# First batch's attention: the mask enters the scores as a product on TensorE, and the exponentials read PSUM

## The chip, the cores and the metric

The kernel runs on one core of one Trainium2 chip. The metric is the time of one execution on the device in microseconds (us), as the median of several runs. The engines go by the names of the profile: PE is TensorE, PEld its weight loads, DVE is VectorE, ACT is ScalarE, POOL is GpSimd, and SP is the engine on whose queue nearly all transfers are issued.

## What is computed

Three stages follow each other: attention over 4 batches of 8 heads (576 positions, 64 wide) in which a position sees a window of 32 positions, plain for the first four heads and with a stride of 4 for the others, and then two feed-forward layers over the 2304 positions.

```python
scores = q @ k.T / sqrt(64)                     # per batch and head, 576 x 576
scores = where(mask, scores, -1e9)              # windows of 32, plain or strided by 4
attn = exp(scores - max(scores)); attn = attn / (sum(attn) + 1e-9)
x = attn @ v                                    # heads side by side: 2304 x 512
x = ((x @ w_a) * (x @ w_b)) @ w_out             # 512 -> 1536 -> 512
h = x @ w_in                                    # 512 -> 2048
out = (max(h, 0) + alpha * min(h, 0)) @ w_out2  # 2048 -> 512
```

The matrices of the two layers arrive as 64-bit floats and are read as integers; the kernel converts them itself.

## The kernel before

**Attention.** A batch is 12 groups (`B`=4 batches, 4 pairs of heads, 3 groups in each). A group is 3 pieces of 64 queries against 96 keys for two heads, so that scores are a tile of 128x288. `Group` holds its operations: `scores` (12 small products into a PSUM tile `sp`), `largest` (DVE: the `scalar_tensor_tensor` of L345 reads `sp`, scales it by 1/8, adds the mask `mk` and writes `st` in SBUF; then the `tensor_reduce` of L351 takes the negated maximum of each row), `exps` (ACT, L356: three exponentials of 128x96 with that maximum as bias and the row's sum as a second output), `weights` (DVE, L363 to L365: reciprocal and product), `transposed` (PE, L372: three transposes into `tp`), `moved` (ACT, L377: copies `tp` to SBUF), `values` (PE, L385: 12 small products into `ap`) and `placed` (DVE, L410: copies `ap` into the layer's input).

**The first batch** stands alone at the start: group i begins at step i, its weights come one step later, its transposes two, its values three. Its `sp` tiles share the tag `at` with two PSUM buffers; `tp` and `ap` have one buffer each (`acc0`, `acc1`). The later three batches run between the products of the first layer; they share banks by twos (`visit_scores`, tile `sa`) and use the same methods of `Group`.

**Fillers.** Before the first step 11 products of zeros (`heat`, L535, 128x512 in bf16) run on PE, and one more in each of the 17 steps of the start. They write a PSUM tile that nobody reads.

**Loads.** `load_qk(n + 3)` is issued after the scores of group n, `load_v(n + 3)` after its values; each has three places in a ring. `queue` and `belt` hold the conversions of weight matrices: a job loads 512 KB of raw words (L194; `in_wab` for the first layer's two matrices, `in_wo` for the third), ACT and DVE make floats of them (L176 to L186) and split them into a high and a low half (L244 on ACT, L247 on DVE), and a store (L258 `wad`, L268 `wod`) keeps a copy. All of these transfers stand on SP's queue.

**The first layer** starts when enough is there: `contract` multiplies the input by a block of `w_a` into `pa` and of `w_b` into `pb`, `expand` multiplies the product by a block of `w_out` into four accumulators; each is made of triples of 128x128x512 products (L452 to L454).

**Order.** The program is written step by step, and a scheduling layer then sets the order of instructions on each engine when the program is built, so that an instruction may stand before one that was written earlier. Each engine, and SP's queue, works through its own order; an instruction that waits holds up all behind it, except that PE loads weights ahead.

Of the kernel before, what the change touches and what calls it, by code (L numbers as in the profile page):

```python
# [12 lines left out]
BF16 = mybir.dt.bfloat16  # L13
U32 = mybir.dt.uint32
I64 = mybir.dt.int64
AF = mybir.ActivationFunctionType
ALU = mybir.AluOpType
AX = mybir.AxisListType

B, H, S, D = 4, 8, 576, 64  # L20
# [6 lines left out]
KT = QT + WINDOW  # L27
NST = S // QT
GS = 3
KS = GS * QT + WINDOW  # L30
NG = NST // GS
NCLS = S // DILATION
NEG = -1.0e9
TILES = [(0, 512), (512, 512), (1024, 512), (1536, 768)]
N_PLAIN = 3

# [3 lines left out]
MASK_OF = {(0, 0): 0, (0, 1): 1, (0, 2): 1, (1, 0): 2, (1, 1): 3, (1, 2): 4}  # L40


def mask_table():
# [4 lines left out]
    for (dil, g), at in MASK_OF.items():  # L48
        for s in range(GS):
# [3 lines left out]
            if dil:  # L53
                ok &= q // NCLS == k // NCLS
            m = np.where(ok, 0.0, NEG)
            out[:QT, at, s], out[QT:, at, s] = m, m
# [4 lines left out]
def tile_kernel(ctx: ExitStack, tc: tile.TileContext, qk, v, mask, wab, wo1, w2, alpha, out):  # L61
    nc = tc.nc
    keep = ctx.enter_context(tc.tile_pool(name="keep", bufs=1))
# [5 lines left out]
    wad = dram.tile([NFA, 128, 1024], F32, name="wad")  # L69
    wsd = dram.tile([NFB // 2, 7, 128, 512], F32, name="wsd")  # L70
    ident = keep.tile([128, 128], F32, name="ident")
    al = keep.tile([128, NFB], F32, name="al")


# [3 lines left out]
    class Ring:  # L78


        def __init__(self, t, first, size, n):
            self.places = [t[:, first + i * size:first + (i + 1) * size] for i in range(n)]
# [5 lines left out]
    def cut(t, first, *dims):  # L88
        size = int(np.prod(dims))
        ap = t[:, first:first + size]  # L90
        if len(dims) == 2:
            ap = ap.rearrange("p (a b) -> p a b", b=dims[1])
        elif len(dims) == 3:
            ap = ap.rearrange("p (a b c) -> p a b c", b=dims[1], c=dims[2])
        return ap
# [17 lines left out]
    sm_ring = Ring(ft, a0 + 4608, 3 * GS, 4)  # L113
    mk = cut(ft, a0 + 4648, 720).bitcast(BF16).rearrange("p (m k) -> p m k", m=5)
# [26 lines left out]
    before, after, now = {}, {}, [0]  # L141

    def at_step(table, k, fn):
        table.setdefault(k, []).append(fn)
# [140 lines left out]
    def load_qk(n):  # L285
        if n < B * NC * NG:
            tqs[n] = t = qk_ring.next()
            nc.sync.dma_start(out=t, in_=qk[n // (NC * NG), n % (NC * NG)])

    def load_v(n):  # L290
        if n < B * NC * NG:
            tvs[n] = t = v_ring.next()[:KT].rearrange("p (s j d) -> p s j d", j=2, d=D)
            nc.sync.dma_start(out=t, in_=v[n // (NC * NG), n % (NC * NG)])

    class Group:


        def __init__(self, b, i, k=None, lag=None, tags=None):
            self.b, self.n, self.pr, self.g = b, b * NC * NG + i, i // NG, i % NG
            self.id = f"{b}_{i}"  # L300
            self.tags = tags
            self.swap = 0
            self.shared = None
            if k is None:
                return
            at_step(before, k, self.scores)
            at_step(after, k + lag[0], self.largest)
            at_step(after, k + lag[1], self.exps)
            at_step(after, k + lag[2], self.weights)
            at_step(before, k + lag[3], self.transposed)  # L310
            at_step(after, k + lag[3], self.moved)
            at_step(before, k + lag[4], self.values)
            at_step(after, k + lag[4], self.placed)
# [2 lines left out]
            tag, bufs = self.tags[n]  # L316
            return ps.tile([128, 512], F32, tag=tag, bufs=bufs, name=f"{what}{self.id}")

        def scores(self):
            Group.scores_of([self])  # L320

        @staticmethod
        def scores_of(groups):


            for a, group in enumerate(groups):
                group.swap = a
                group.tq = tqs.pop(group.n)
                group.sp = group.psum(0, "sp") if group.shared is None else group.shared
            for s in range(GS):  # L330
                for group in groups:
                    for j in range(2):
                        half, to = (slice(x * 64, (x + 1) * 64) for x in (j, j ^ group.swap))
                        nc.tensor.matmul(
                            group.sp[to, s * KT:(s + 1) * KT],
                            lhsT=group.tq[half, s * QT:(s + 1) * QT],
                            rhs=group.tq[half, GS * QT + s * QT:GS * QT + s * QT + KT],
                            start=True, stop=True,
                        )
            for group in groups:  # L340
                load_qk(group.n + 3)

        def largest(self):
            self.st = st_ring.next().rearrange("p (s k) -> p s k", k=KT)
            nc.vector.scalar_tensor_tensor(  # L345
                out=self.st.rearrange("p s k -> p (s k)"), in0=self.sp[:, :GS * KT], scalar=1.0 / float(D) ** 0.5,
                in1=mk[:, MASK_OF[int(self.pr >= 2), self.g]], op0=ALU.mult, op1=ALU.add,
            )
            self.sp = None
            self.sm = sm_ring.next().rearrange("p (a s) -> p a s", s=GS)  # L350
            nc.vector.tensor_reduce(out=self.sm[:, 0], in_=self.st, axis=AX.X, op=ALU.max, negate=True)  # L351

        def exps(self):
            self.et = et_ring.next().rearrange("p (s k) -> p s k", k=KT)
            for s in range(GS):
                nc.scalar.activation(  # L356
                    self.et[:, s], self.st[:, s], AF.Exp, bias=self.sm[:, 0, s:s + 1], accum_out=self.sm[:, 1, s:s + 1]
                )
            self.st = None

# [112 lines left out]
    def bank(tag):  # L473
        return ps.tile([128, 512], F32, tag=tag, name=tag)
# [22 lines left out]
    load_qk(1)  # L497
    load_v(1)
    make_identity(nc, ident)
    xn[0], xn[1] = cut(ft, 0, 4, 512), cut(ft, 2048, 4, 512)  # L500

    def more():
# [6 lines left out]
    lag = (0, 0, 1, 2, 3)  # L509
# [8 lines left out]
    k = 5  # L518
# [7 lines left out]
                job_o(k, job[3])  # L526
        k += 2 if k < n_start else 1

    zeros = keep.tile([128, 512], BF16, name="zeros")
    nc.vector.memset(zeros, 0.0)  # L530
    idle = bank("pb")

    def heat(n):
        for _ in range(n):
            nc.tensor.matmul(idle, lhsT=zeros[:, :128], rhs=zeros, start=True, stop=True)  # L535

    heat(11)
    for _ in range(n_start):
        step(lambda: heat(1))
    nc.sync.dma_start(out=al, in_=alpha)  # L540
# [37 lines left out]
    for t in range(3):  # L578
# [3 lines left out]
        for j in range(len(pairs) + 1):  # L582
            k = slots[2 * j] if j < len(pairs) else slots[-1] + 2
# [65 lines left out]
    k = start_of[N_PLAIN - 1]  # L649
# [25 lines left out]
    for t, (t0, n) in enumerate(TILES[:N_PLAIN]):  # L675
# [3 lines left out]
        for f in range(NFA):  # L679
# [11 lines left out]
            k = now[0]  # L691
# [233 lines left out]
```

## Time and profile before

| | before |
|---|---|
| median of 3 runs | 913.97 us (912.05 to 916.38) |
| the profiled execution | 919.15 us |
| its span in the profile | 917.1 us |
| PE busy | 895.0 us (98%) |
| DVE busy | 617.4 us (67%) |
| ACT busy | 415.2 us (45%) |
| mean granted TensorE clock over the span | 0.988 of full |

The profiled execution lies 5.2 us above the median. 2.05 us of it lie outside the span. Busy shares are means over the whole program: the first batch's attention is over within some 45 us of the start, and only there, and in the some 25 us after it, PE is idle for more than moments at a time. A busy PE is not a PE at full speed: two clock levels are granted, 2.4 GHz (1.00 in the tables) and 1.2 GHz (0.50).

### The profile page before, as it was taken

How to read it: one execution, taken by the hardware profiler on the slowest of the kernel's cores; microseconds unless marked ns; L12 is line 12 of the kernel's file. 1: busy time of each engine (PE TensorE's matmuls, PEld its weight loads, DVE VectorE, ACT ScalarE, POOL GpSimd, SP SyncE). 2: the span in 40 equal slices, each digit the busy share in tenths (PEclk: the TensorE clock that was granted, in tenths of full speed). 3: DMA queues.
4: the chain of work that ended last, by engine and by line, in shares of the span. 5: the costliest groups of instructions: out<-in, count | busy, mean ns of one | idle time of the engine just before them, and what ended most of it. 6: DMA issues, size and time to landing. Idle time of an engine off the chain costs nothing.

```text
span 917.1 us, 15187 instructions
## 1 busy us (share of the span) xinstructions
PE 895.0 (98%) x5572; PEld 810.7 (88%) x5572; DVE 617.4 (67%) x1317; ACT 415.2 (45%) x967; POOL 0.7 (0%) x6
## 2 busy tenths in 40 slices
PE   8979999999999999999999998999999999999998
PEld 5658888888777778899999998999999999999998
DVE  5788897656766776579877588759555575555442
ACT  5787886545545544345445356224222242222221
POOL 0000000000000000000000000000000000000000
PEclk9899999999999999999999999999999999999999
DMA  7788894687778663663322987557445445454200
GB/s 206 221 297 298 307 336 177 226 267 262 228 240 282 216 204 122 205 206 131 124 93 68 329 288 274 156 157 239 118 118 150 127 115 157 115 146 123 71 35 34
DMA packets 76585, 171.24 MB, mean 187 GB/s; under 512 B 8672, under 2 KB 23776, under 8 KB 76512
## 3 DMA queue, kind: packets, MB, share of 16 engines
q1 hardware_dynamic: 76512, 170.28, 57.5%
q8 instruction: 44, 0.72, 0.3%
q14 instruction: 29, 0.24, 0.1%
HBM read 133.55 MB, written 36.70 MB: 186 GB/s over the span
## 4 chain that ended last, share of the span: by engine, by line
PE 78%; DMA 10%; DVE 5%; ACT 4%; issue 1%; SPq 1%; ACTq 0%; DVEq 0%
PE at L711 12%; PE pb L711 8%; PE pa L711 8%; PE accB L453 7%; PE accB L454 7%; PE accB L452 7%; DMA ft<-in_w 5%; PE accA L452 4%; PE accA L453 4%; PE accA L454 4%; PE pa L452 2%; PE pb L452 2%; PE pb L453 2%; PE pa L454 2%; PE pb L454 2%; PE pa L453 2%
## 5 line engine op out<-in xcount | busy, mean ns | idle before, releaser
L244 ACT CAST rt<-ft 128x512 fp32r<-128x512 f32 (+2 forms) x288 | 159.3, 561 | 280.4 <-PE accB L454 169.1
L247 DVE TENSOR_TENSOR rt<-ft,rt 128x512 fp32r<-128x512 f32 (+2 forms) x288 | 174.8, 613 | 135.0 <-ACT rt L244 121.1
L711 PE MATMUL at<-rt 128*128 128x384 f32 x648 | 130.7, 334 | 1.2 <-DMA rt<-wsd 1.2
L453 PE MATMUL accB<-rt 128*128 128x384 f32 x384 | 128.7, 335 | 0.2 <-DVE rt L247 0.2
L454 PE MATMUL accB<-rt 128*128 128x384 f32 x384 | 128.7, 335 | 0.0
L452 PE MATMUL accB<-rt 128*128 128x384 f32 x384 | 127.8, 335 | 0.0
L711 PEld LDWEIGHTS at<-rt 128*128 128x128 f32 x648 | 113.9, 188 | 1.7 <-DMA rt<-wsd 1.6
L452 PE MATMUL accA<-rt 128*128 128x512 f32 (+1 forms) x240 | 90.0, 379 | 5.7 <-ACT rt L244 4.5
L725 ACT COPY ft<-at 128x384 f32<-128x384 f32 x108 | 51.8, 480 | 89.4 <-PE at L711 87.3
L453 PE MATMUL accA<-rt 128*128 128x512 f32 (+1 forms) x240 | 89.3, 372 | 0.7 <-DVE rt L247 0.7
L711 PE MATMUL pb<-rt 128*128 128x384 f32 x432 | 87.2, 336 | 2.8 <-DVE ft L722 2.8
L454 PE MATMUL accA<-rt 128*128 128x512 f32 (+1 forms) x240 | 88.9, 370 | 0.0
L711 PE MATMUL pa<-rt 128*128 128x384 f32 x432 | 88.1, 337 | 0.0
L711 PEld LDWEIGHTS pb<-rt 128*128 128x128 f32 x432 | 75.6, 188 | 4.6 <-DVE ft L722 4.6
L711 PEld LDWEIGHTS pa<-rt 128*128 128x128 f32 x432 | 76.7, 189 | 0.1
L453 PEld LDWEIGHTS accB<-rt 128*128 128x128 f32 x384 | 72.3, 188 | 0.6 <-DVE rt L247 0.5
L454 PEld LDWEIGHTS accB<-rt 128*128 128x128 f32 x384 | 72.4, 188 | 0.0
L452 PEld LDWEIGHTS accB<-rt 128*128 128x128 f32 x384 | 72.3, 188 | 0.0
L183 DVE SCALAR_TENSOR_TENSOR ft<-ft 128x512 uint32<-128x512 uint32 x68 | 46.8, 688 | 34.9 <-ACT ft L179 34.5
L176 ACT ACTIVATE ft<-ft 128x512 f32<-128x512 f32 x68 | 45.7, 672 | 46.9 <-DMA ft<-in_w 43.3
L356 ACT ACTIVATE ft<-ft 128x96 f32<-128x96 f32 x144 | 52.1, 363 | 20.0 <-DVE ft L351 20.0
L722 DVE TENSOR_TENSOR ft<-ft,pb 128x384 f32<-128x384 f32 x72 | 39.7, 551 | 29.5 <-ACT ft L725 29.2
(80 smaller groups left out, 1351.3 us busy)
## 6 DMA issues: line engine op xcount, KB each, us to landing
rt<-wsd SPq DMA_DIRECT2D x168, 256.0 KB, 2.9
rt<-wod SPq DMA_DIRECT2D x48, 512.0 KB, 4.2
ft<-in_w SPq DMA_DIRECT2D x32, 512.0 KB, 5.1
wsd<-rt SPq DMA_DIRECT2D x56, 256.0 KB, 2.6
ft<-in_wab SPq DMA_DIRECT2D x24, 512.0 KB, 5.4
ft<-in_qk SPq DMA_DIRECT2D x48, 208.0 KB, 4.3
ft<-in_v SPq DMA_DIRECT2D x48, 144.0 KB, 4.2
wad<-ft SPq DMA_DIRECT2D x24, 256.0 KB, 4.7
```

The costliest lines, as they stand in the source:

```text
L176: nc.scalar.activation(f, high.bitcast(F32), AF.Abs, scale=2.0 ** -112)
L183: nc.vector.scalar_tensor_tensor(out=fi, in0=fi, scalar=3, in1=low, op0=ALU.logical_shift_left, op1=ALU.bitwise_or)
L244: hi_eng.copy(hi, x)
L247: lo_eng.tensor_tensor(out=lo, in0=x, in1=hi.bitcast(F32), op=ALU.subtract)
L356: nc.scalar.activation(self.et[:, s], self.st[:, s], AF.Exp, bias=self.sm[:, 0, s:s + 1], accum_out=self.sm[:, 1, s:s + 1])
L452: nc.tensor.matmul(acc, lhsT=wh, rhs=rh, start=first, stop=False)
L453: nc.tensor.matmul(acc, lhsT=wh, rhs=rl, start=False, stop=False)
L454: nc.tensor.matmul(acc, lhsT=wl, rhs=rh, start=False, stop=last)
L711: nc.tensor.matmul(acc[:, :HT], lhsT=a, rhs=x[:, b, c], start=start and c == k == 0, stop=c == 1 and k == 2, skip_group_check=not start,)
L722: nc.vector.tensor_tensor(out=out, in0=x, in1=acc[:, :HT], op=ALU.add)
L725: nc.scalar.copy(out, acc[:, :HT])
```

## The change

Only the first batch changes. The mask no longer enters on DVE: for each of the 12 groups a product of a bf16 identity (`ident_b`) and the mask's 288 columns (bf16, now -8e9 where masked, since the scale of 1/8 comes later) is written into `sp` first, and the 12 score products add to it. The maximum is taken by a `tensor_reduce` straight from `sp` and then scaled by a small `tensor_scalar` of 128x3; L345's pass is gone. The exponentials read `sp` in PSUM, with the scale as an argument, so a bank of `at` is held until the third exponential is done, where it was free after L345. The later batches keep their path (with the other value of `NEG`). The fillers have 384 columns where they had 512, and 14 stand ahead of the first step where 11 stood; `zeros` now shares a tile `few` with `ident_b`, which POOL casts from `ident`.

```diff
-NEG = -1.0e9
+NEG = -8.0e9
+SCALE = 1.0 / float(D) ** 0.5
...
+    few = keep.tile([128, 512], BF16, name="few")
+    ident_b, zeros = few[:, :128], few[:, 128:]
...
-            self.shared = None
+            self.sp = self.shared = None
+            self.scale = 1.0 if k is None else SCALE
             if k is None:
                 return
-            at_step(before, k, self.scores)
-            at_step(after, k + lag[0], self.largest)
+            at_step(before, k, self.masked_scores)
+            at_step(after, k + lag[0], self.largest_masked)
...
-        def scores(self):
+        def masked_scores(self):
+
+            self.sp = self.psum(0, "sp")
+            nc.tensor.matmul(
+                self.sp[:, :GS * KT], lhsT=ident_b, rhs=mk[:, MASK_OF[int(self.pr >= 2), self.g]],
+                start=True, stop=True,
+            )
             Group.scores_of([self])
+
+        def largest_masked(self):
+            self.st = self.sp[:, :GS * KT].rearrange("p (s k) -> p s k", k=KT)
+            self.sm = sm_ring.next().rearrange("p (a s) -> p a s", s=GS)
+            nc.vector.tensor_reduce(out=self.sm[:, 0], in_=self.st, axis=AX.X, op=ALU.max, negate=True)
+            nc.vector.tensor_scalar(self.sm[:, 0], self.sm[:, 0], SCALE, None, op0=ALU.mult)
+            self.sp = None
...
-                group.sp = group.psum(0, "sp") if group.shared is None else group.shared
+                new = group.sp is None
+                if new:
+                    group.sp = group.shared
...
-                            start=True, stop=True,
+                            start=new, stop=True, skip_group_check=not new,
...
                 nc.scalar.activation(
-                    self.et[:, s], self.st[:, s], AF.Exp, bias=self.sm[:, 0, s:s + 1], accum_out=self.sm[:, 1, s:s + 1]
+                    self.et[:, s], self.st[:, s], AF.Exp, scale=self.scale, bias=self.sm[:, 0, s:s + 1],
+                    accum_out=self.sm[:, 1, s:s + 1],
                 )
...
+    nc.gpsimd.tensor_copy(ident_b, ident)
...
-            nc.tensor.matmul(idle, lhsT=zeros[:, :128], rhs=zeros, start=True, stop=True)
+            nc.tensor.matmul(idle[:, :384], lhsT=zeros[:, :128], rhs=zeros, start=True, stop=True)
 
-    heat(11)
+    heat(14)
```

The built order differs in the start only; from about PE's 770th instruction of some 5050 on it is the same. Three places follow, each before and then after; `sp_0` and so on are the score tiles of groups 0, 1, 2, and what stands in brackets are the engines or transfers that the row waits for.

PE, from the last fillers ahead of the first scores to the third group's scores, before:

```order
L535 MATMUL pb<-zeros 128x512
L334 MATMUL sp_0_97<-ft 64x96 [waits DMAHW1_49]
L334 MATMUL sp_0_97<-ft 64x96 x5
L535 LDWEIGHTS zeros
L535 MATMUL pb<-zeros 128x512
L334 MATMUL sp_1_111<-ft 64x96 [waits DMAHW3_49]
L334 MATMUL sp_1_111<-ft 64x96 x5
L535 LDWEIGHTS zeros
L535 MATMUL pb<-zeros 128x512
L334 MATMUL sp_2_132<-ft 64x96 [waits DMAHW5_49,DVE_49]
```

The same stretch after (`few` holds zeros and the identity; L326 is the mask's product, L353 are the scores, L392 the first group's transposes):

```order
L555 MATMUL pb<-few 128x384
L326 LDWEIGHTS few [waits Pool_49]
L326 MATMUL sp_0_101<-ft,few 128x288 [waits DMAHW0_49]
L353 MATMUL sp_0_101<-ft 64x96 [waits DMAHW1_49]
L353 MATMUL sp_0_101<-ft 64x96 x5
L326 LDWEIGHTS few
L326 MATMUL sp_1_116<-ft,few 128x288
L353 MATMUL sp_1_116<-ft 64x96 [waits DMAHW3_49]
L353 MATMUL sp_1_116<-ft 64x96 x5
L326 LDWEIGHTS few [waits DVE_49]
L326 MATMUL sp_2_138<-ft,few 128x288 [waits Activation_49]
L353 MATMUL sp_2_138<-ft 64x96 [waits DMAHW5_49]
```

All 31 fillers now stand ahead of the first scores, where 17 of 28 stood between the groups; the third group's tile waits for ACT, where it waited for DVE.

ACT, its first rows, before (L356 are the exponentials, L377 the copy of `tp`):

```order
L356 ACT_TABLE_LOAD
L356 ACTIVATE ft<-ft 128x96 [waits DVE_49]
L356 ACTIVATE ft<-ft 128x96 x2
L356 ACTIVATE ft<-ft 128x96 [waits DVE_49]
L356 ACTIVATE ft<-ft 128x96 x2
```

And after (L375 are the exponentials):

```order
L375 ACT_TABLE_LOAD [waits DVE_49]
L375 ACTIVATE ft<-sp_0_101,ft 128x96 [waits PE_49]
L375 ACTIVATE ft<-sp_0_101,ft 128x96 x2
L375 ACTIVATE ft<-sp_1_116,ft 128x96 [waits DVE_49,PE_49]
L375 ACTIVATE ft<-sp_1_116,ft 128x96 x2
```

The first exponential now has two waits, one of which stands ahead of the load of ACT's tables; that wait is for the scaled maximum of group 0.

SP's queue from the fourth group's `in_qk` load to the first raw weights, before:

```order
L288 DMA ft<-in_qk 128x416 [waits DMAHW1_49,PE_49]
L288 DMA ft<-in_qk 128x416 [waits DMAHW3_49,DMAHW2_49,PE_49]
L288 DMA ft<-in_qk 128x416 [waits DMAHW5_49,PE_49]
L288 DMA ft<-in_qk 128x416 [waits DMAHW4_49,DMAHW1_49,PE_49]
L288 DMA ft<-in_qk 128x416 [waits DMAHW2_49,PE_49]
L288 DMA ft<-in_qk 128x416 [waits DMAHW6_49,DMAHW3_49,PE_49]
L194 DMA ft<-in_wab 128x512 [waits DMAHW7_49]
```

And after (L291 is `load_qk`, L296 `load_v`, L197 the raw load):

```order
L291 DMA ft<-in_qk 128x416 [waits DMAHW1_49,PE_49]
L291 DMA ft<-in_qk 128x416 [waits DMAHW3_49,DMAHW2_49,PE_49]
L291 DMA ft<-in_qk 128x416 [waits DMAHW5_49,PE_49]
L296 DMA ft<-in_v 96x384 [waits DMAHW4_49,PE_49]
L291 DMA ft<-in_qk 128x416 [waits DMAHW1_49,PE_49]
L296 DMA ft<-in_v 96x384 [waits DMAHW6_49,PE_49]
L291 DMA ft<-in_qk 128x416 [waits DMAHW7_49,DMAHW2_49,PE_49]
L296 DMA ft<-in_v 96x384 [waits DMAHW0_49,PE_49]
L291 DMA ft<-in_qk 128x416 [waits DMAHW3_49,PE_49]
L197 DMA ft<-in_wab 128x512
```

Six `in_qk` loads stand ahead of the first raw weights in both; after, three `in_v` loads, which wait for the values of groups 0 to 2, stand there too.

## Rows read from the trace of the kernel before

**Rows 1.** Page, part 2: busy tenths and granted clock in 40 slices.

```profile
PE   8979999999999999999999998999999999999998
PEclk9899999999999999999999999999999999999999
```

**Rows 2.** Stretches, PE alone: from:to, length, busy (instructions), granted clock, DMA share, GB/s.

```profile
18.50:21.90 3.40, 2.20 (x34) 0.99 0.60 172
22.00:27.80 5.80, 5.80 (x55) 0.50 0.66 197
...
32.20:36.00 3.80, 3.18 (x60) 1.00 0.63 197
49.20:52.60 3.40, 1.73 (x10) 1.00 0.96 300
63.00:66.20 3.20, 0.97 (x3) 1.00 1.06 349
...
80.00:540.00 460.00, 455.21 (x2864) 1.00 0.64 217
```

**Rows 3.** Chain of waits, first 90 us: start, length, engine, tile, line.

```profile
1.19 4.29 PE pb L535 x11
5.48 0.64 PE sp L334 x12
...
22.76 1.47 PE sp L334 x14
24.23 0.84 PE ap L385 x12
25.06 0.81 PE tp L372 x3
...
27.85 0.73 PE pa L452
...
29.01 0.43 PE pa L454
...
34.05 5.66 DMA ft<-in_wab
```

**Rows 4.** Timeline of PE: start, length, instructions, [idle before, releaser].

```profile
21.38 0.57 PE L385 MATMUL ap<-ft 96*64 96x64 f32 x12 [0.62 <-ACT ft L377]
...
44.29 0.57 PE L385 MATMUL ap<-ft 96*64 96x64 f32 x12
...
67.31 1.65 PE L452 MATMUL accA<-rt 128*128 128x512 f32 x3 [3.07 <-ACT rt L244]
```

**Rows 5.** Timeline of ACT, the table load and two exponentials three apart.

```profile
0.74 1.28 ACT L356 ACT_TABLE_LOAD   x1 [0.74 <-PEq L917]
7.14 0.37 ACT L356 ACTIVATE ft<-ft 128x96 f32<-128x96 f32 x1 [5.12 <-DVE ft L351]
...
8.23 0.36 ACT L356 ACTIVATE ft<-ft 128x96 f32<-128x96 f32 x1
```

**Rows 6.** Timeline of DVE, group 0's mask and maximum, and a small operation.

```profile
6.17 0.46 DVE L345 SCALAR_TENSOR_TENSOR ft<-sp,ft 128x288 f32<-128x288 f32 x1 [5.04 <-PE sp L334]
6.66 0.45 DVE L351 TENSOR_REDUCE ft<-ft 128x3 f32<-128x288 f32 x1
...
8.36 0.17 DVE L363 TENSOR_SCALAR ft<-ft 128x3 f32<-128x3 f32 x1 [0.28 <-ACT ft L356]
```

**Rows 7.** Timeline of SP's queue: issues of raw weights and a store of converted ones.

```profile
13.89 0.43 SPq L194 DMA_DIRECT2D ft<-in_wab  x1
...
28.38 0.48 SPq L194 DMA_DIRECT2D ft<-in_wab  x1
...
45.32 0.38 SPq L194 DMA_DIRECT2D ft<-in_wo  x1
...
54.20 0.33 SPq L268 DMA_DIRECT2D wod<-rt  x1
54.59 1.26 SPq L194 DMA_DIRECT2D ft<-in_wab  x2
```

More of the change, by code (lines that the diff above doesn't have):

```diff
@@ L345, in largest @@
             nc.vector.scalar_tensor_tensor(
-                out=self.st.rearrange("p s k -> p (s k)"), in0=self.sp[:, :GS * KT], scalar=1.0 / float(D) ** 0.5,
+                out=self.st.rearrange("p s k -> p (s k)"), in0=self.sp[:, :GS * KT], scalar=SCALE,
                 in1=mk[:, MASK_OF[int(self.pr >= 2), self.g]], op0=ALU.mult, op1=ALU.add,
@@ L527, in tile_kernel @@
         k += 2 if k < n_start else 1
-    zeros = keep.tile([128, 512], BF16, name="zeros")
     nc.vector.memset(zeros, 0.0)
```

## The prediction

> **What bounds the kernel now.** I read the page's slices first: PE is at nine tenths or more nearly everywhere, and the dents lie in the first three slices [rows 1]. From 80 to 540 us PE is busy 455.21 of 460 us at full clock [rows 2], so what the start costs is paid in full at the end. Then the chain of waits over the first 90 us, which is the stage of the change. It goes through PE's attention products, then through loads of raw weights, as the one that moves from 34.05 for 5.66 us [rows 3]. PE starves a last time before 67.31, where a weight cast on ACT releases it after 3.07 us [rows 4]; behind that moment it has a backlog. So a shift of 67.31 is the change of the time.
>
> What sets 67.31? The load issued on SP at 54.59 stands behind the store at 54.20, which waits for the conversion of a matrix loaded at 45.32 [rows 7]. That load stands in the queue behind the `in_v` load that follows the last group's values, which run on PE at 44.29 [rows 4]. The earlier weight loads, at 13.89 and 28.38 [rows 7], stand behind loads that wait for scores and values too. The start is therefore paced by how fast PE gets through the first batch, and the thing to watch there is the granted clock. It is full until about 21.9, although PE is busy 2.20 of 3.40 us before that [rows 2], with idle pieces like the 0.62 us at 21.38 [rows 4]. Then it is at half, and it stays there through 22.0 to 27.8, where PE has small attention products without a pause [rows 2]. The first large products (`pa`) begin at 27.85 [rows 3], and by 32.2 the clock is full again [rows 2].
>
> **The change, part by part.** *Fillers.* 11 products of 512 columns took 4.29 us [rows 3]; a large product of 512 columns at half clock takes 0.43 [rows 3], so most of the 11 ran at half and the last few at full. All 31 fillers now stand ahead of the first scores. At 384 columns one takes 0.32 us at half clock and some 0.17 at full: about 3.6 us for the first 11, 3.4 for the other 20, from 1.19 to 8.2. The first scores, at 5.48 before [rows 3], begin 2.8 us later. The other 17 fillers, which kept PE busy between the groups, are gone from there.
>
> *Mask product.* Its 288 columns are 288/512 of 0.43 us at half clock, 0.24 us, and 0.12 at full; 12 of them are 1.4 to 2.9 us on PE. Its weights load beside other products, or add a tenth each; I take nothing.
>
> *DVE.* Twelve passes of 0.46 us leave, twelve small operations of 0.17 us come [rows 6]. The maximum reads PSUM: between 0 and the 0.46 of the PSUM-reading pass, most likely unchanged at 0.45 [rows 6]. DVE gains some 3.5 us of work, but was waiting for PE here. Exponentials out of PSUM are not in these rows; I take the 1.09 us for three that rows 5 show (7.14 to 8.23), with 0.05 either way for each: the clock matters far more.
>
> *Table load.* Before, ACT loads its tables at 0.74, while nothing else goes on, for 1.28 us [rows 5]. Now a wait for group 0's scaled maximum stands ahead of it. With scores 0 done at 8.2 + 0.12 + 0.64 = 8.96 and scores 1 at 9.72, the maximum begins at 9.0, its scaling ends 0.49 + 0.17 later, at 9.7; the table load ends at 11.0, the three exponentials at 12.1. The third group's mask product waits for them, since there are two banks, and transposes and values of group 0 need the same exponentials. PE has nothing from 9.72 to 12.15: **2.4 us of idleness**, in 3.4 us of which it is busy for 1.0 with small products.
>
> On this load the Trainium skill says more (ScalarE: Activation LUTs, What ACT_TABLE_LOAD costs): a switch of tables costs about 2.66 us with the drain behind it. Nothing follows the load closely in this trace, so it cannot tell. By that figure the idle stretch would be 3.8 us and the forecast below 1.4 us higher.
>
> *The clock.* I expect it to fall in or right after this gap. Before, it fell with PE busy 2.20 of 3.40 us, and again around 66.2, after 0.97 of 3.20 [rows 2]. It held through 49.2 to 52.6, where PE is busy for only 1.73 of 3.40 [rows 2], but with large products; the new gap has small ones around it and no filler. Once at half it should stay, as in 22.0 to 27.8, until `pa` begins.
>
> *The first batch at half clock.* A group costs PE 0.24 for the mask, 12/14 of 1.47 = 1.26 for scores, 0.81 for transposes and 0.84 for values [rows 3]: 3.15 us, more than its exponentials (1.1) and copy on ACT, so PE sets the pace. From 12.15 to the first `pa` there stand on PE 9 masks and scores, 8 transposes and 7 values: 13.5 + 6.5 + 5.9 = 25.9. `pa` begins at 38.0 where it began at 27.85 [rows 3], 10.2 us later. The third weight load, behind values 6, goes at about 36.2, where it went at 28.38 [rows 7].
>
> *What is given back.* From `pa` to the last values 16.4 us passed before (27.85 to 44.29), partly in waits for weight loads; after, two raw loads are long there and converted. I walk on: the clock is full some 4.3 us after `pa` begins, at 42.3; values 8 follow at 43.5 and release the fourth load, at 44.5; ACT converts the third (landed at 41.9, by the 5.66 us of rows 3) until 46.0, copies and exponentials of groups 9 to 11 follow by 48.5, the fourth load's first two passes by 51, and the last values come at 51.6. That is 7.3 us after 44.29, with 2 us of doubt each way. The raw load of 45.32 and all that hang on it move along: its store (54.20) to 61.5, the next load (54.59) to 61.9, PE's last starvation from 67.31 to 74.6. Later PE idleness (4.8 us of 80 to 540) could give back a microsecond.
>
> *Sum.* 919.15 + 7.3 = 926.5 for a profiled execution. That lies 5.2 above the median of the runs, so **921.3 us** against 913.97.
>
> **The rivals.** *The clock holds, and the change is faster.* If the gap does not lower it, a group costs PE 1.6 us (0.12 + 0.64 + about half of 0.81 and 0.84). The two banks then set some 1.9 us a group: scores 5 end at 18.4, the first raw load goes at 18.9; values 6 run at 25.5, the last values at about 36. The loads are then paced by load and conversion, some 8 us each pair: third at 27, fourth at 30.8, the one of 45.32 at 39.5, so 5.8 us earlier: 908.2. For it speaks 49.2 to 52.6 [rows 2], and that the work just before the gap is dense fillers at full clock. Against it speaks 21.9, which fell over less. A rule stands beside this: the Trainium skill (TensorE: Matmul & The Clock Gate, Why this matters for your kernels) warns only of long idle gaps between bursts, and no gap here would be long by it; by that rule the time is this rival's. The trace disagrees: at 21.9 the clock fell over gaps of about 0.6 us.
>
> *The clock falls, but late.* It survives the gap and falls near 22, when ACT waits for the first raw load with exponentials behind it. By then scores 8 are done and five to six values, as before; `pa` begins near 28.3 against 27.85, the time is 914, within 2.
>
> *Less is moved than it seems.* If the tables' load did not wait, the gap would be 1.1 us. Then the second rival and the first are the likely ones, with 914 or 907. I give this no chance of its own, since the order shows the wait.
>
> *Worse.* The table load takes longer than its row, or conversions and attention stand in each other's way on ACT while PE is at half: 10 us or more, 924 and up.
>
> **How the numbers follow.** Early fall 0.70 (917 to 926), of which the worst case is 0.07; late fall 0.15 (912 to 917); no fall 0.15 (906 to 911). The range from 911 to 927 leaves out most of the no-fall case and a tail above, about 0.2. A half per cent is 4.6 us, about what a measurement of this kernel can tell from no change. Slower by more (over 918.5): most of the first case, 0.62. Faster by more (under 909.4): two thirds of the last, 0.10. Within: 0.28.
>
> **What would show it.** In the trace after: fillers without a break until about 8.2; the table load at about 9.7 instead of 0.74; PE idle some 2.4 us before the third mask product; a granted clock at half from 12 to 15 us on until about 42; the first `pa` near 38, the last values near 52, the raw load that was issued at 54.59 near 62. Wrong would be: a clock at full past 16 us, then I expect `pa` at 29 or earlier and no loss; or the delay of `pa` without a delay of the last starvation, then the weights, and not the attention, paced the start.

## The result and the profile after

| | before | after |
|---|---|---|
| median | 913.41 us (20 executions, 908.93 to 916.77) | 920.19 us (20 executions, 912.35 to 930.25) |
| the profiled execution | 919.15 us | 920.89 us |
| its span | 917.1 us | 919.1 us |
| mean granted clock over the span | 0.988 | 0.996 |

The changed kernel is slower by 6.8 us in the medians; the ratio is 1.0064 [1.0046, 1.0081]. (The ratios here and below leave out executions far above the fastest of the same kernel: the five above 926 us here, which experiment 7 shows to belong to the kernel, one of 1245.83 us in experiment 8, and one of 1193.6 us of the kernel before in the session of experiments 5 to 7.) The forecast was 921.3 us, 7.3 us slower. The times of after lie in two groups: twelve executions from 912.35 to 920.89 us with a mean clock of 0.993 to 1.000, and eight from 923.28 to 930.25 us with 0.976 to 0.983. Before has no second group. The profiled execution is of the faster group.

The page's slices (answer to [rows 1]): beside two dents of PE in the start there are two, in the slices of 230 to 253 and of 299 to 322 us, that before does not have.

```profile
PE   8989999999899899999999999999999999999998
PEclk9999999999999999999999999999999999999999
```

Stretches of PE (from:to, length, busy, granted clock, DMA share, GB/s; answer to [rows 2]). PE is busy 1.06 us of the 3.40 ahead of 13.0; then the clock is at half, but only to 16.8, and full again although nothing but attention products runs. From 80 to 540 us PE is busy 4.5 us less than before did there, 2.5 of them between 225 and 255 (28.78 us in before).

```profile
9.60:13.00 3.40, 1.06 (x18) 1.00 0.44 125
13.40:16.80 3.40, 3.40 (x34) 0.50 0.22 67
16.80:30.00 13.20, 12.57 (x172) 1.00 0.73 225
...
225.00:255.00 30.00, 26.24 (x178) 1.00 0.67 222
80.00:540.00 460.00, 450.67 (x2838) 1.00 0.63 217
```

The stretch in before, with the busy time of PE, PEld, DVE, ACT and POOL:

```profile
225.00:255.00 30.00, 28.78 (x194) 23.09 (x193) 21.75 (x60) 17.16 (x49) 0.00 (x0) 1.00 0.74 251
```

The chain of waits, first 90 us (start, length, what; answer to [rows 3]): the fillers in one piece, then the table load, later two loads of raw weights.

```profile
1.12 7.87 PE pb L555 x31
...
10.55 1.28 ACT L375
...
26.23 5.36 DMA ft<-in_wab
...
58.41 7.36 DMA ft<-in_wab
```

Timeline of PE (start, length, instructions, [idle before, releaser]; answer to [rows 4]): the first mask product and scores, the wait for the first exponentials, the first `pa`, the last values, the last starvation, and two waits at 252 and 254 us.

```profile
8.83 0.29 PE L326 MATMUL sp<-ft,few 128*128 128x288 bf16 x1
9.05 0.71 PE L353 MATMUL sp<-ft 64*64 64x96 f32 x12
...
12.97 0.28 PE L326 MATMUL sp<-ft,few 128*128 128x288 bf16 x1 [2.34 <-ACT ft L375]
...
32.32 0.50 PE L472 MATMUL pa<-rt 128*128 128x512 f32 x1
...
45.15 0.57 PE L405 MATMUL ap<-ft 96*64 96x64 f32 x12
...
71.68 0.85 PE L392 MATMUL tp<-ident,ft 128*96 128x128 f32 x3 [1.33 <-DVE ft L385]
...
252.51 0.51 PE L392 MATMUL tp<-ident,ft 128*96 128x128 f32 x3 [1.97 <-DVE ft L383]
254.22 0.51 PE L392 MATMUL tp<-ident,ft 128*96 128x128 f32 x3 [1.20 <-ACT ft L708]
```

Timeline of ACT (answer to [rows 5]) and of DVE (answer to [rows 6]): the table load waits for group 0's scaled maximum; an exponential out of PSUM takes 0.34, and one starts every 0.32 us. At 246.32 ACT has waited 7.76 us for a load; in before it had waited 4.52 us, as the last fence of the three shows.

```profile
10.55 1.28 ACT L375 ACT_TABLE_LOAD   x1 [10.55 <-DVE ft L336]
11.85 0.34 ACT L375 ACTIVATE ft<-sp,ft 128x96 f32<-128x96 f32 x1
...
12.81 0.34 ACT L375 ACTIVATE ft<-sp,ft 128x96 f32<-128x96 f32 x1
...
246.32 0.67 ACT L179 ACTIVATE ft<-ft 128x512 f32<-128x512 f32 x1 [7.76 <-DMA ft<-in_w]
```

```profile
9.81 0.46 DVE L335 TENSOR_REDUCE ft<-sp 128x3 f32<-128x288 f32 x1 [8.74 <-PE sp L353]
10.30 0.17 DVE L336 TENSOR_SCALAR ft<-ft 128x3 f32<-128x3 f32 x1
```

```profile
244.07 0.67 ACT L176 ACTIVATE ft<-ft 128x512 f32<-128x512 f32 x1 [4.52 <-DMA ft<-in_w]
```

SP's queue (answer to [rows 7]): the same loads as there. The first is 8.5 us later than before, the one of `in_wo` 1.4 and the pair 3.8.

```profile
22.43 0.42 SPq L197 DMA_DIRECT2D ft<-in_wab  x1
...
31.79 0.43 SPq L197 DMA_DIRECT2D ft<-in_wab  x1
...
46.69 0.35 SPq L197 DMA_DIRECT2D ft<-in_wo  x1
...
57.97 0.38 SPq L271 DMA_DIRECT2D wod<-rt  x1
58.41 1.41 SPq L197 DMA_DIRECT2D ft<-in_wab  x2
```

So two things were left to explain: why the time has two groups, and what is lost near 250 us, where nothing was changed.

### The profile page after: what moved, and what is told of

It reads as the page before. It is cut to its first block, busy times and chain, and to the rows that moved or that the text cites. A ratio compares the mean times of both kernels' runs of the same rounds, so it can differ in the third digit from the quotient of the medians.

```text
span 919.1 us, 15210 instructions
## 1 busy us (share of the span) xinstructions
PE 893.1 (97%) x5587; PEld 808.9 (88%) x5587; DVE 614.5 (67%) x1317; ACT 414.1 (45%) x967; POOL 1.0 (0%) x7
## 4 chain that ended last, share of the span: by engine, by line
PE 66%; DMA 15%; DVE 10%; ACT 6%; issue 2%; SPq 1%; ACTq 0%; DVEq 0%
PE at L731 11%; PE pb L731 7%; PE pa L731 7%; PE accB L473 7%; PE accB L474 7%; PE accB L472 7%; DMA ft<-in_w 6%; DMA ft<-in_wab 4%; PE accA L472 3%; PE accA L473 3%; PE accA L474 3%; DVE rt L250 2%; DMA wsd<-rt 2%; DVE ft L186 2%; ACT ft L375 2%
## 5 line engine op out<-in xcount | busy, mean ns | idle before, releaser
L472 PE MATMUL pa<-rt 128*128 128x512 f32 x140 | 56.9, 406 | 1.5 <-ACT rt L247 1.5
```

The costliest lines, as they stand in the source:

```text
L472: nc.tensor.matmul(acc, lhsT=wh, rhs=rh, start=first, stop=False)
```

## The experiments

Ratios are against the kernel before, run on the same chip in the same session.

**1. The change once more** (`after_again`, no edit).

> The changed kernel once more. Theory G (the gap): the 2.3 us in which PE has nothing after the second group's scores lowers the granted clock, and in a part of the executions it then stays at half until the first large products; the times then lie in two groups, about 926 us with a mean clock of 0.976 to 0.983 and about 917 us with 0.993 to 1.0. Theory F (the fillers): what costs is that all 31 fillers stand ahead of the first scores, 3.4 us for every execution; then the times have one group near 917 to 921, whatever the clock.

Measured: 922.56 us median (918.76 to 930.65), ratio 1.0113 [1.0074, 1.0151]. Three executions lie at 918.76 to 920.60 us (clock 0.991 to 0.996), two at 925.46 and 930.65 (0.983 and 0.978); one at 924.53 with 0.990 fits neither group of Theory G. Theory F, with one group up to 921 us, fails. The profiled execution (919.34 us) has the clock at half from 12.9 to 16.3, again right behind the 2.3 us wait, and from 251.8 to 255.3. The fall at the start repeats; the long stay at half is not in the profiled execution.

**2. The exponential table early** (`table_early`).

```diff
+    warm = keep.tile([128, 1], F32, name="warm")
+    nc.vector.memset(warm, 0.0)
+    nc.scalar.activation(warm, warm, AF.Exp)
```

> The changed kernel with one added exponential of 128x1 on a zeroed tile at the very start, so that ACT loads its tables while the fillers run. Theory G: the gap shrinks by 1.28 us to about 1.1 us, the clock falls less often or not at all, the group near 926 us vanishes, and the time is 913 to 917 (ratio to before 1.000 to 1.004). Theory F: only the 1.28 us are gained at most, 918 to 920 (1.005 to 1.007).

Measured: 915.84 us (911.59 to 918.33), ratio 1.0027 [1.0009, 1.0046], every execution at a clock of 0.992 or more: the slow group is gone. The table loads at 0.73, and the wait ahead of the third mask product is less than half of 2.34 us (timeline of PE of this kernel):

```profile
10.81 0.28 PE L326 MATMUL sp<-ft,few 128*128 128x288 bf16 x1 [1.06 <-ACT ft L375]
```

In its trace the clock is full from 4.7 to 45.7. So the waiting table load makes the slow group. But the kernel is still 2.5 us slower than before, with the clock kept.

**3. No fillers between the groups** (`fill_14`).

```diff
-        step(lambda: heat(1))
+        step()
```

> The changed kernel without the 17 fillers of the steps: 14 of 384 columns stand ahead of the first scores, which begin some 2.8 us earlier. Theory G: the gap is as long as before, with less dense work ahead of it, so that the clock falls at least as often: 920 us or more (ratio 1.006 or more). Theory F: 2.8 us are gained in every execution, about 917 (1.003).

Measured: 917.82 us (913.14 to 924.47), ratio 1.0063 [1.0028, 1.0097]. The first mask product starts at 5.58 instead of 8.83, and the wait of 2.34 us stays. In the trace, which is of the slowest of the seven executions, the clock falls more often (to half at 10.5, 34.4, 51.5 and twice later); of the seven mean clocks only one, 0.981, is as low as in the slow group of after. Inconclusive by itself: the ratio is what Theory G expected, the median nearly that of Theory F, and the earlier start and the clock work against each other.

**4. The fillers ahead, in the kernel before** (`before_fill_front`).

```diff
-    heat(11)
+    heat(28)
     for _ in range(n_start):
-        step(lambda: heat(1))
+        step()
```

> The kernel before with its 28 fillers of 512 columns all ahead of the first scores and none between the groups; masks, maximum and exponentials as before. Theory F: the first scores begin some 4 us later and the time is 917 to 918 (ratio 1.004 to 1.005). Theory G: there is no gap from a table load, so the clock holds at least through the first groups, and the late beginning is made up where loads pace the start: 912 to 916 (1.000 to 1.003).

Measured: 916.59 us (912.61 to 921.0), ratio 1.0039 [1.0019, 1.0058], clock 0.991 or more. The place of the fillers costs some 3.6 us without anything else of the change. That lies between the two ranges, nearer to Theory F, while the clock held as Theory G says. Its stretch at 240 us is as in before: ACT waits 4.17 us for that load, PE not at all for `tp`.

**The loss near 250 us.** ACT's wait of 7.76 us in after and 8.03 us in `table_early` is for a pair of `in_w` loads of 512 KB. A transfer reports from 16 parts. For this pair in after, the 15th part of each came 4.3 and 5.0 us behind the issue, but the last one 7.7 and 8.5. All four runs so far with the mask product (after twice, `table_early`, `fill_14`) show this late part there (3.4 to 3.7 us behind the 15th); in the two without it, before and `before_fill_front`, the last part is under 0.15 us late. What stands out is a packet of 8 KB on queue q14, named instruction in the profile, 0.7 us behind the issue of the pair in the four; in before it comes 3.6 us behind it and in `before_fill_front` 5.0. The DMA view of after over 238.5 to 239.5, when the pair is issued (queue: packets, MB, share; then name, KB, us to landing), and of before over 239.3 to 240.5, without a row of q14:

```profile
q14 instruction: 1, 0.01, 2.0%
...
ft<-in_w SPq DMA_DIRECT2D x2, 512.0 KB, 8.1
```

```profile
ft<-in_w SPq DMA_DIRECT2D x2, 512.0 KB, 4.9
```

The programs differ in one more thing: the traces have 971 instructions of SyncE in before, 969 in `before_fill_front` and 973 in the four (the expectation below counts two more in each), since other waits stand among its first transfers, and ahead of the pair 334, 332 and 336. In after, packets of q14 come when SyncE has started 82, 210 and 338 instructions, 128 apart, and the third is the one here. If the packet is SyncE's own code, two instructions move it. The Trainium skill (DMA: Bandwidth & Descriptors, Queues, rings and completion order) says that row 14 of the queues carries such refills, and that a DMA engine takes turns between its rows; the trace agrees on the queue; no run here shows the turns. The next four kernels add drains to SyncE in a place where they wait for nothing, and leave every other instruction in its order:

```diff
         raws = [load_raw(w2[2 * i + j, 0], raw_b_ring) for j in range(2)]
+        for _ in range(2 if i == 0 else 0):
+            tc.keep_in_program_order(nc.sync.drain())
```

**5. Two instructions more in the kernel before** (`before_code_2`).

> The kernel before with two instructions more on SyncE (two drains, which wait for nothing there) behind the first w2 conversion step's loads, ahead of the in_w loads of 239 us; the order of everything else is the same, and SyncE then holds 975 instructions as the changed kernel does (973 before). Theory C (the code load): an 8 KB packet of instructions on queue q14 falls 0.7 us behind the issue of in_w (3.6 us in before), one of that load's 16 parts comes 3.3 to 3.7 us after the other 15, ACT's wait for in_w there grows from 4.5 to 7.5-8.1 us, PE waits some 2 us for DVE's and 1.2 us for ACT's part of the tp products near 252 us, and the time goes from 913.4 to 915.5-917 (ratio 1.002 to 1.004). Theory M (the mask products, the few tile in memory, or the earlier start of the loads): nothing of this appears, in_w lands in under 5.5 us, ratio 0.999 to 1.001.

Measured: 916.81 us (913.61 to 919.63), ratio 1.0031 [1.0009, 1.0053]. Theory C to the number: the q14 packet comes 0.7 us behind the pair, the late part lags 3.3 us, ACT waits 7.67 us and PE 1.86 and 1.20. Behind PE's waits the granted clock is at half as well, for 6.8 us in this trace (247.5 to 254.3) and for 3.4 us in `after_again`, `table_early` and `fill_14`, but not in after; how much of the loss is idleness and how much is clock was not separated. Its DMA view over 232.8 to 233.8, and its timelines of ACT and PE:

```profile
q14 instruction: 1, 0.01, 2.0%
...
ft<-in_w SPq DMA_DIRECT2D x2, 512.0 KB, 8.0
```

```profile
240.59 0.66 ACT L176 ACTIVATE ft<-ft 128x512 f32<-128x512 f32 x1 [7.67 <-DMA ft<-in_w]
```

```profile
246.77 0.50 PE L374 MATMUL tp<-ident,ft 128*96 128x128 f32 x3 [1.86 <-DVE ft L365]
248.48 0.85 PE L374 MATMUL tp<-ident,ft 128*96 128x128 f32 x3 [1.20 <-ACT ft L690]
```

**6. Six and twelve more in `table_early`** (`table_early_code_6`, `table_early_code_12`).

> The changed kernel with the early exponential (as table_early) and six drains on SyncE behind the first w2 conversion step's loads, so that SyncE's code load falls some six instructions earlier against the in_w loads. Theory C: it comes before in_w's issue at 234 us, in_w lands in 4.5 to 6.5 us instead of 8.0 and 8.7, PE's waits of 2.2 and 1.2 us near 250 us go, and the time falls from 915.8 to 912.5-914.5 (ratio 0.999 to 1.001); what the late part delays instead is the wod or wsd transfer ahead, at up to 1 us. Theory M: in_w still takes 8 us and the time stays at 915-916.5 (ratio 1.002 to 1.004).

> As table_early_code_6, with twelve drains: the code load falls twelve instructions earlier against the in_w loads. Theory C: in_w at 234 us in 4.5 to 6.5 us, time 912.5 to 914.5 (ratio 0.999 to 1.001), and if the late part always costs something, the two shifts differ by the transfer that they hit. Theory M: as table_early, 915-916.5 (1.002 to 1.004).

Measured: 914.12 us (910.26 to 917.11), ratio 1.0003 [0.9982, 1.0024], and 913.61 us (908.89 to 917.64), ratio 0.9995 [0.9976, 1.0014]. The intervals overlap that of `table_early`; the traces show the difference. The packet comes 3.2 and 9.6 us ahead of the pair, which lands in 4.4 to 5.2 us, and PE's two waits are gone. Timeline of ACT of `table_early_code_12`:

```profile
239.41 0.67 ACT L179 ACTIVATE ft<-ft 128x512 f32<-128x512 f32 x1 [4.29 <-DMA ft<-in_w]
```

Theory M, by which the mask products or the tile `few` delay the load, fails in both directions: the loss comes without them (experiment 5) and goes with them. With that, the change with an early table is as fast as before.

**7. Six more in the change itself** (`after_code_6`).

> The changed kernel itself with the six drains, and nothing else. Theory C: the late in_w part at 238 us goes and with it 2 to 3 us, so that the executions at a clock of 0.993 and more come at 913.5 to 917 (912 to 921 without the drains), while the group at 923 to 930 stays, some 2 us lower, since the gap ahead of the first exponentials is as it was; ratio 1.003 to 1.006. Theory M: 916-921 and 923-930 as without them, ratio 1.006 to 1.011.

Measured: 918.03 us (913.87 to 927.26), ratio 1.0056 [1.0025, 1.0087]: seven executions from 913.87 to 918.15 at a clock of 0.992 to 0.998, five from 921.81 to 927.26 at 0.980 to 0.983. Both groups are lower (medians 916.85 and 923.57 us, against 917.88 and 926.90 in after), and both are still there. Against `table_early_code_6` the waiting table load costs 0.0053 or 3.9 us in the medians. The profiled execution is the one of 927.26 us, of the slow group. Its stretches of PE, and the first `pa` and the last values in its timeline:

```profile
8.30:11.90 3.60, 1.67 (x27) 1.00 0.35 102
11.90:15.30 3.40, 2.99 (x23) 0.52 0.16 47
15.30:42.60 27.30, 27.18 (x210) 0.50 0.50 154
42.60:59.70 17.10, 14.43 (x138) 0.99 0.77 249
```

```profile
40.78 0.79 PE L474 MATMUL pa<-rt 128*128 128x512 f32 x1
...
54.10 0.57 PE L407 MATMUL ap<-ft 96*64 96x64 f32 x12
```

The clock is at half from 12.1 to 42.8. Here it does what the forecast said: down at the gap, at half under small products that leave PE no pause, and full again after `pa` has begun.

**8. The shift in the kernel before** (`before_code_12`, the drains of experiment 6).

> The kernel before with twelve drains on SyncE behind the first w2 conversion step's loads, all else in its order. It tells whether the shift of the code load that helped the changed kernel is worth something by itself. Theory C (only a code load right behind in_w's issue costs): in before it comes 3.6 us behind in_w and its late part (0.8 us) is hidden, so 912.5 to 914.5, ratio 0.9985 to 1.0005. Rival: any distance to in_w helps, ratio 0.996 to 0.998.

Measured: 912.62 us (910.26 to 915.15, and one execution of 1245.83), ratio 0.9992 [0.9973, 1.001]. In before the code load costs nothing to speak of.

**9. Fewer fillers ahead, and some between the groups** (`few_ahead_code_12`, `pinned_code_12`, `pinned_more_code_12`). All three kernels are `table_early_code_12` with 16 fillers ahead of the first scores; the first has no others, the second has one pinned to its place in each step, the third three in each of the first five steps and one in each later one. The edit of the second against `table_early_code_12`, cut:

```diff
-    heat(14)
+    heat(16)
     for _ in range(n_start):
-        step(lambda: heat(1))
+        step(lambda: heat(1, True))
...
+            if pinned:
+                tc.keep_in_program_order(mm)
```

> The changed kernel with the early exponential and twelve drains (as table_early_code_12), and of the 31 fillers only 16, all ahead of the first scores; none in the steps. Theory F (the fillers ahead hold up the start): the first scores start at 5.2 to 6 us instead of 9.05, pa and the conversions come 2 to 3 us earlier, 910.5 to 912.5, ratio 0.996 to 0.9985. Theory G (the clock needs the fillers): with small products alone from 6 us on the granted clock falls to half somewhere in 8 to 40 us, and the time is 913 to 918 with some executions above 920, ratio 0.999 to 1.005.

> As few_ahead_code_12, with the other fillers pinned to their places in the written order, one ahead of each step's scores. Theory F: scores from 5.2 to 6 us, one filler of 0.25 us in each group hidden in PE's waits of 0.4 to 1 us there, 910 to 912.5, ratio 0.996 to 0.9985, and a clock above 0.99 in all executions. Rival: the pinned fillers stand in front of products that are ready and take 17 x 0.25 = 4 us back, 913 to 915, ratio 0.9995 to 1.002.

> As pinned_code_12, with three fillers in each of the first five steps instead of one, as the kernel before has up to five between its first groups. Theory F: they lie in the waits for the first exponentials, 910 to 913, ratio 0.996 to 0.999. Rival: 10 x 0.25 = 2.5 us longer than pinned_code_12.

Measured: 910.53 us, ratio 0.9964 [0.9942, 0.9986]; 908.55 us (905.49 to 912.08), ratio 0.9953 [0.9933, 0.9973]; 911.2 us, ratio 0.9971 [0.9952, 0.9989]. Theory F holds: the first mask product starts 2.8 to 2.9 us earlier than in `table_early_code_12`, and with one pinned filler in each step some 4 us are gained (0.9953 against 0.9995, each against before in its own session), more than I expected. Theory G fails for `few_ahead_code_12`: its trace has the clock full from 6.9 to 44.5, although no filler stands there. The intervals of the first two kernels overlap, so what is shown is that fillers ahead cost; whether one in each step helps is not. Ten fillers more came out 2.65 us slower in the medians and 2.0 in the means, with overlapping intervals; that is near the last rival, but 911.2 us also lies in the range of its Theory F. Timeline of PE of `pinned_code_12`:

```profile
1.16 5.20 PE L560 MATMUL pb<-few 128*128 128x384 bf16 x16 [1.16 <-DVE few L555]
6.20 0.29 PE L328 MATMUL sp<-ft,few 128*128 128x288 bf16 x1
...
9.06 0.28 PE L328 MATMUL sp<-ft,few 128*128 128x288 bf16 x1 [0.64 <-ACT ft L377]
```

This is the version that beats both kernels, by 0.5% against before. How much of that is the mask product is not shown: the kernel before was not run with fillers of this length, number and place, and ten fillers more or less move the time by some 2 us. In the change as written, the fillers ahead, the code load and the waiting table load take back more than the 0.5%.

## Why the prediction was right, and where it was not

The sign, the size and the range held; that the median came so near is luck. The forecast of 921.3 us lies between the two groups of times (none of the 20 executions is between 920.89 and 923.28), and of what slows the faster group it had the late start but not the code load.

Adding up, by the ratios: the change with an early table, the code moved away and 16 fillers ahead is 4.3 us faster than before (0.9953 of 913.41); all fillers ahead cost 3.8 (0.9953 to 0.9995); the code load 2.2 to 2.9 (1.0027 against 1.0003 and 0.9995); the waiting table load 3.9 in the medians and 4.8 by the ratios (experiment 7). The sum is 5.6 to 7.2 where the medians gave 6.8. The first three are steps from before to `table_early` and give its 2.5 us by construction; what is tested is that the last one fills the rest. By the six executions of experiment 1 the rest would be larger (1.0113).

*Fillers ahead*: right. They ended at 8.99, not 8.2; the clock rose at 6.6 in this execution, and in `table_early`, where it rose at 4.7, they ended at 8.10. The delay of the first scores, 3.4 us against 5.41, was taken as part of one long shift; the experiments show it as a cost of its own.

*Mask product*: priced too low. From its start to that of the scores behind it 0.22 us pass at full clock (8.83 to 9.05) and some 0.36 at half in `after_code_6`, not 0.12 and 0.24.

*DVE, exponentials*: right. The maximum out of PSUM took 0.46 (0.45 forecast), its scaling 0.17, three exponentials 0.96 us (11.85 to 12.81; 1.09 forecast).

*Table load*: right. PE waited 2.34 us (2.4 forecast). On the figure of the Trainium skill (ScalarE: Activation LUTs, What ACT_TABLE_LOAD costs), 2.66 us with a drain behind the load: the load took 1.28 us and the first exponential began 0.02 us after it, so the larger gap of 3.8 us did not come.

*The clock falls in or after the gap*: right in every trace with that wait (at half from 13.4, 12.9, 12.1 and 10.5). The Trainium skill (TensorE: Matmul & The Clock Gate, Why this matters for your kernels) warns of long idle gaps between bursts; the traces do not agree that a gap must be long: 2.34 us were enough.

*Once at half it stays until `pa`*: this is the step that failed. In the profiled execution of after it came back after 3.4 us, under the same small products. A full clock past 16 us was the prediction's own sign of being wrong; but `pa` came at 32.32, not at 29 or earlier, and a loss remained. By the mean clocks, the long stay is the minority, eight of 20; one trace, that of `after_code_6`, shows it. There the walk was close and somewhat low: `pa` at 40.78 (38.0), last values at 54.10 (51.6). The term that was too small is a group at half clock: its scores mostly stood in two halves of 0.83 us, together 1.66 and not 1.26, and with the mask product a group took some 3.55 and not 3.15 us.

*From the profiled execution to the median*: also wrong. The before that I had profiled was itself unusual: its clock of 0.988, with half from 21.8 to 32.1, is below the 0.992 to 0.998 of nearly all others. In `before_code_12`, the same kernel up to the drains, the clock is full from 7.0 to 65.1, `pa` begins at 26.56 and the last values at 41.75. I subtracted 5.2 us from a forecast for the slow group. 926.5 us was right for that group (923.28 to 930.25), and 921.3 met the median of the mixture.

*The rival with the clock held*: one execution of the 20 had a mean clock of 1.000 (912.35 us, not 908.2), and in the faster group the clock is at half only briefly, so the case nearly exists; its size was wrong. The profiled execution has the last values at 45.15, not 36: a group takes 2.1 us at full clock, not 1.9, the first weight load goes at 22.43, not 18.9, and the three later loads that I walked through are 4.8 to 7.2 us behind that walk. With the code load in it, this group ends slower than before, not 5.8 us faster.

*A shift of the last starvation is the change of the time*: held, but for the code load. From `before_code_12` to `after_code_6`, where that load costs nothing, PE's last wait of over a microsecond in the first 100 us moved by 15.4 us (65.52 to 80.90) and the span by 15.8 (909.7 to 925.5).

*What no step had*: the 2 to 3 us of the code load near 240 us. That later idleness could give back a microsecond had the wrong sign.

What stays open: why PE is idle some 2 us more than in before between 80 and 540 us outside 225 to 255 (part of it recurs: a wait of 0.70 to 0.94 us for ACT ahead of products into the tile `sa` of the later batches, between 308 and 328 us, in seven of the ten traces with the mask product and in none of the four without it); why the clock recovers after 3.4 us in one execution and after 30.7 in another; and where all of the 3.6 us of experiment 4 go, since its last values come only 0.6 us later than in `before_code_12`.

## What to carry to other kernels

When an operation's input changes, look at what stands in front of its first use: a table load takes over the wait of the first instruction that needs it, and one throwaway exponential at the start took it away. A change in one stage can move the count of instructions on every queue, so compare the far stages too, and when a load there lands late by one part of 16, see whether an instruction packet fell into it; a few idle instructions on SyncE told that apart. A single profiled execution with a mean clock below the others' is no base for a forecast.

## What the runs showed of the hardware that I had not expected

- **A piece of SyncE's code can hold up a transfer.** When a packet of 8 KB on q14, which takes 0.31 to 0.39 us, fell 0.7 us behind the issue of a pair of 512 KB loads, one part of each came 3.3 to 3.7 us late, in all five runs (four kernels) where it did; at 3.6 us behind, or 3.2 ahead, the last part was 0.25 us late or less. Two instructions on SyncE decided it, at 2.8 us of the time (ratio 1.0031 [1.0009, 1.0053]). Why one part loses so much more than the packet takes is not shown.
- **The same gap, two outcomes.** PE waited 2.34 us in after and in `after_code_6`. In the first the clock was at half for 3.4 us with PE busy throughout (13.40 to 16.80) and then full under attention products; in the second, where the end of the wait lay in the first 3.4 us (busy 2.99), it was at half for 30.7 us with PE as busy later on (27.18 of 27.30 us).
- **Exponentials out of PSUM are no slower**: one every 0.32 us, where [rows 5] has 0.36 each out of SBUF.
